# Wider small matmuls, three constant matmuls a chunk and later ScalarE routing calls in a fused RWKV and top-1 expert kernel

## The chip, the cores and the metric

The kernel runs on one core of a Trainium2 chip. The metric is the device time of one execution in microseconds (us). TensorE, VectorE, ScalarE, GpSimd (POOL) and the DMA issuer SP each run their own instruction stream in order and meet through semaphores.

## The reference

Two stages. The first is linear attention with a decaying state (RWKV) over r, k, v of shape (4 batches, 8 heads, 768 positions, 48), in float32:

```
for t in range(S):
    cur = einsum('bhd,bhe->bhde', u * k[t], v[t])
    y[t] = einsum('bhd,bhde->bhe', r[t], state + cur)
    state = w[:, None] * state + einsum('bhd,bhe->bhde', k[t], v[t])
```

The second takes y as x (3072 tokens of 384) into a mixture of 8 experts with one expert a token:

```
logits = x @ w_gate;  e = argmax(logits);  p = softmax(logits)[e]
o = sigmoid(x @ w_output_gate)[e]
out = p * o * (relu(x @ w1[e]) @ w2[e])      # w1: 384 x 1024, w2: 1024 x 384
```

## The kernel before, in words

The attention is cut into NT = 24 chunks of 128 positions: six steps in time, four batches in each, so that chunk i follows chunk i - 4 of its own batch. In a chunk the heads are held as four pairs; a chunk is split again into two halves of 64 positions, so nearly every matmul works on 64 by 64 or 48 by 64 corners of the 128 by 128 array, four of them (or two) side by side.

For one chunk these pieces of work exist, with the names that the code gives them:

- `load` (L1219): four DMAs on SP bring r, k (by head) and k, v (by token) into the tile `rkv`. `scale` (VectorE, L249), `keys` (POOL, L255) and `product` (POOL, L262) put the decay powers in.
- `scores` (L279): 16 float32 matmuls, 64 moving columns each, into columns 0 to 255 of the two banks `pa`. `causal` (VectorE, L285) masks them into `A`.
- `state` (L306): 16 matmuls with 48 moving columns, into columns 256 to 447 of the same two banks. `carry` (L316) adds the old state on VectorE (L323, or L320 for the first) and multiplies by the decay on POOL (L324): the tile `T`.
- `inter` (L340, 48 columns) and `intra` (L350, 48 columns) accumulate into the pair of banks `y`: what the state gives, and what the chunk itself gives. There is one pair, so the next chunk's `inter` waits for `output`.
- `coefs` (L360): eight matmuls, 128 rows by 64 columns of the array, whose moving operand repeats two columns 20 times: 40 columns. ScalarE copies eight of them out (`cs`, L1321), and `bonus` (L369) is eight ScalarE calls that multiply v by them.
- `output` (L376): VectorE adds y and the bonus to x; SP stores x. 
- `logits_t` (L413, three transposes of x into the one bank of tag `lg`, and ScalarE's copy `xT`, L415) and `logits_into` (L423): six matmuls whose moving operand repeats 16 gate columns three times, 48 in all. ScalarE copies 16 columns out (L431).

Each float32 matmul stands in the profile as two instructions.

The routing runs by groups of chunks (5, 5, 4, 4 and 6). `group` (L439) is a generator: it issues an operation or two and yields what kind of step comes next. In a chunk `micro` (L1306) is called at seven or more places; each adds a credit and lets VectorE steps run while credit lasts, and `tensor_slot` (L1313) lets a TensorE step run. The side generator `weighting` (L481) is advanced inside the same steps. ScalarE's three calls of a group are issued wherever the program is when it comes to them: the exponential `ex` (L464), the gate's exponential `en` (L492) and the row product `rhs` (L570). The last group runs after the attention, beside the first expert.

The order of every engine's stream in the attention is the order in which the code is written (`manual_schedule`). In the loop from L1354 one turn issues: product, scale, carry, keys, routing steps, the next chunk's `coefs` with ScalarE's copy, the logits of chunk i - 2, the transposes of x of chunk i - 1, the bonus calls of chunk i + 1, intra and output of chunk i, a load, state of chunk i + 2, scores of chunk i + 1, carry, causal, inter of chunk i + 1, routing steps. From chunk 18 on two pieces a turn split the first expert's weights on ScalarE and POOL (L798). Behind the loop come the experts, all on full 128 by 128 weights with up to 512 moving columns.

The kernel already holds a `warm` tile of bf16 ones, used for matmuls ahead of the attention (L114) and one in the loop's second turn (L1325).

Of the kernel before, what the change touches and what calls it, by code (L numbers as in the profile page):

```python
# [8 lines left out]
F32 = mybir.dt.float32  # L9
# [16 lines left out]
IN = RKW + 2 * DM  # L26
# [23 lines left out]
V, P, SPLIT = "vector", "tensor", "split"  # L50
# [3 lines left out]
BUDGETS = [[0, 0.25], [16, 0.3]]  # L54
# [177 lines left out]
class Attention:  # L232
    def __init__(self, tc, ctx, ps, k, load, x_d):
        self.tc, self.k, self.ps = tc, k, ps
        self.load, self.x_d = load, x_d
        self.pw = ctx.enter_context(tc.tile_pool(name="att_w", bufs=2))
        self.st, self.T, self.vc, self.A, self.rk, self.y = {}, {}, {}, {}, {}, {}
        self.pa = {}

    def view(self, i):  # L240
        t = self.load(i)
        return t[:, :RKW].rearrange("p (n c q t) -> p n c q t", n=2, c=2, q=NP), t[:, RKW : RKW + DM], t[:, RKW + DM :].rearrange("p (h d) -> p h d", h=H)
# [49 lines left out]
    def state(self, i):  # L292
        if i >= NT:
            return
        nc = self.tc.nc
        _, kn, vt = self.view(i)
# [14 lines left out]
    def carry(self, i, c):  # L311
        if i >= NT or (c == 1 and self.last(i)):
            return
        nc, k = self.tc.nc, self.k
        a = NP * HB
        U = self.pa[:, c, a : a + NP * D].rearrange("p (q e) -> p q e", q=NP)  # L316
        decay = k.w64.unsqueeze(2).to_broadcast((C, NP, D))
        T = self.pw.tile([C, NP, D], F32, name=f"T{c}", bufs=(3, B + 2)[c])
        if i < B and c == 0:
            nc.vector.tensor_mul(T, U, decay)  # L320
        else:
            T1 = self.pw.tile([C, NP, D], F32, name="Ts")
            nc.vector.tensor_add(T1, U, self.T[i, 0] if c else self.T[i - B, 1])  # L323
            nc.gpsimd.tensor_mul(T, T1, decay)  # L324
        self.T[i, c] = T

    def inter(self, i):
        if i >= NT:
            return
        nc = self.tc.nc  # L330
        rk = self.view(i)[0]
        self.y[i] = y = self.banks("ps_y", "y")
        T = [None if i < B else self.T[i - B, 1], self.T[i, 0]]
        for q in range(NP):
            for j in range(2):
                rows = slice(HB * j, HB * j + D)
                for c in range(2):
                    half = slice(HB * c, HB * (c + 1))
                    if T[c] is not None:
                        nc.tensor.matmul(y[half, j, D * q : D * (q + 1)], rk[rows, 0, c, q, :], T[c][rows, q, :], start=(q == 0), stop=False, skip_group_check=True)  # L340

    def intra(self, i):
        nc = self.tc.nc
        vt, A, y = self.view(i)[2], self.A.pop(i), self.y[i]
        for q in range(NP):
            for j in range(2):
                for c in range(2):
                    rows = slice(HB * c, HB * (c + 1))
                    o = y[rows, j, D * q : D * (q + 1)]
                    nc.tensor.matmul(o, A[rows, j, q, :], vt[rows, 2 * q + j, :], start=(i < B and c == 0 and q == 0), stop=(q == NP - 1), skip_group_check=True)  # L350

    def coefs(self, i, lg):
        if i >= NT:
            return
        rk = self.rk.pop(i)
        for q in range(NP):
            for n in range(2):
                half = slice(HB * n, HB * (n + 1))
                o = lg[half, : 60 * E].rearrange("p (a b) -> p a b", b=3 * E)[:, :, 2 * E + 2 * q : 2 * E + 2 * (q + 1)]
                self.tc.nc.tensor.matmul(o, rk[:, n, q, :], self.k.uw[:, q, :].unsqueeze(1).to_broadcast((C, 20, 2)), start=True, stop=True, skip_group_check=True)  # L360
# [11 lines left out]
    def output(self, i):  # L372
        nc = self.tc.nc
        x = self.pw.tile([C, DM], F32, name="x")
        xq, vq = (t.rearrange("p (q j) d -> p j q d", j=2) for t in (x.rearrange("p (h d) -> p h d", d=D), self.vc.pop(i)))
        nc.vector.tensor_add(xq, self.y.pop(i)[:, :, : NP * D].rearrange("p j (q d) -> p j q d", d=D), vq)  # L376
        nc.sync.dma_start(self.x_d[i * C : (i + 1) * C, :], x)
        return x


class Router:
# [36 lines left out]
    def logits_into(self, pl, xT):  # L418
        for j in range(KC):
            for n in range(2):  # L420
                half = slice(HB * n, HB * (n + 1))
                o = pl[half, : 9 * E].rearrange("p (a b) -> p a b", b=3 * E)[:, :, : 2 * E]
                self.tc.nc.tensor.matmul(o, xT[:, j, half], self.wg32[:, j, :].unsqueeze(1).to_broadcast((C, 3, 2 * E)), start=(j == 0), stop=(j == KC - 1), skip_group_check=True)  # L423
# [15 lines left out]
    def group(self, ps, w, lg, i0, G, closing, last):  # L439
# [24 lines left out]
        nc.scalar.activation(ex, d, AF.Exp)  # L464
# [16 lines left out]
        def weighting():  # L481
            z8 = mk("z8", E)
            nc.vector.tensor_mul(z8, oh, g)
            se = mk("se")
            nc.vector.tensor_reduce(out=se, in_=ex, axis=AX.X, op=ALU.add)
            yield
            z = mk("z")
            nc.vector.tensor_reduce(out=z, in_=z8, axis=AX.X, op=ALU.add)
            nc.vector.tensor_scalar(se, se, 1e-9, None, op0=ALU.add)
            yield  # L490
# [4 lines left out]
            yield  # L495
            den = mk("den")
            nc.vector.scalar_tensor_tensor(den, en, 1.0, se, op0=ALU.add, op1=ALU.mult)
            yield
            scale = self.scale[:, cols]
            nc.vector.reciprocal(scale, den)  # L500
            yield
            rest = scale
            for i in range(3):
                nc.vector.tensor_copy(parts[:, i], rest)
                yield
                if i < 2:
                    nxt = mk(f"rest{i}")
                    nc.vector.tensor_sub(nxt, rest, parts[:, i])
                    rest = nxt
                    yield  # L510
# [12 lines left out]
        next(side, None)  # L523
        yield V
# [10 lines left out]
        next(side, None)  # L535
        yield V
        rank = self.rank[:, cols]
        nc.vector.tensor_reduce(out=rank, in_=rk, axis=AX.X, op=ALU.add)
        next(side, None)
        yield V  # L540
        ge = mk("ge", NQ)
        nc.vector.tensor_tensor(ge, bc(rank, NQ), rep(k.thr, NQ), op=ALU.is_ge)
        next(side, None)
        yield V
        q = mk("q")
        nc.vector.tensor_reduce(out=q, in_=ge, axis=AX.X, op=ALU.add)
        next(side, None)
        yield V
# [4 lines left out]
        next(side, None)  # L553
# [8 lines left out]
        next(side, None)  # L562
# [3 lines left out]
        next(side, None)  # L566
# [3 lines left out]
        nc.scalar.activation(rhs[:, :, 1], sel, AF.Copy, scale=k.row1)  # L570
        tab = self.tab

# [17 lines left out]
        if last:  # L590
# [25 lines left out]
            for _ in weighting():  # L616
                yield V
# [15 lines left out]
        for _ in side:  # L633
            yield V
        for i in range(3):
            yield Slot(0.2)
            columns(i)
        yield P
# [559 lines left out]
def rwkv_top1_moe(ctx, tc, rkv, wu, wg, w1, w2, r, kk, v, w, u, out):  # L1198
# [11 lines left out]
    with ExitStack() as actx:  # L1210
# [105 lines left out]

        def strips(i, cs):
            if i < NT:
                lg = ps.tile([C, 512], F32, name="ps_cf", tag="lg", bufs=1)
                att.coefs(i, lg)  # L1320
                nc.scalar.copy(cs, lg[:, 2 * E : 3 * E])  # L1321
# [5 lines left out]
        make_tables(tc, ps, k)  # L1327
        att.scale(0)
# [25 lines left out]
        for i in range(NT):  # L1354
# [106 lines left out]
def laid_out(r, k, v, w, u, moe_w_gate, moe_w_output_gate, moe_w1, moe_w2):  # L1461
# [12 lines left out]
    for i, a in enumerate((w, u)):  # L1474
# [3 lines left out]
        "rkv": np.concatenate([heads(r), heads(k), tokens(k), tokens(v)], axis=2),  # L1478
# [27 lines left out]
```

## Time and profile before

| | us |
|---|---|
| median of three runs | 422.16 |
| lowest and highest of them | 419.49, 426.5 |
| the profiled execution | 421.16 |
| its span, first to last instruction | 419.2 |
| TensorE busy (matmul) in the span | 373.1 |
| VectorE, ScalarE, POOL busy | 234.9, 173.2, 156.3 |
| mean granted TensorE clock | 0.892 |

The span is the time from the first to the last instruction of the program; the profiled execution's own time is 1.96 us longer. The granted clock is the share of full speed that TensorE's clock was given: 1.00 is its level of 2.4 GHz and 0.50 its level of 1.2 GHz. In the profile's rows PE is TensorE's matmul stream and PEld its weight loads; DVE is VectorE, ACT ScalarE; `<-` names what ended an engine's wait, and "issue" is a wait that nothing in the profile explains. A matmul's end is modelled.

### The profile page before, as it was taken

How to read it: one execution, taken by the hardware profiler on the slowest of the kernel's cores; microseconds unless marked ns; L12 is line 12 of the kernel's file. 1: busy time of each engine (PE TensorE's matmuls, PEld its weight loads, DVE VectorE, ACT ScalarE, POOL GpSimd, SP SyncE). 2: the span in 40 equal slices, each digit the busy share in tenths (PEclk: the TensorE clock that was granted, in tenths of full speed). 3: DMA queues.
4: the chain of work that ended last, by engine and by line, in shares of the span. 5: the costliest groups of instructions: out<-in, count | busy, mean ns of one | idle time of the engine just before them, and what ended most of it. 6: DMA issues, size and time to landing. Idle time of an engine off the chain costs nothing. (4 is left out here: it accounts for less than half of the span.)

```text
span 419.2 us, 12629 instructions
## 1 busy us (share of the span) xinstructions
PE 373.1 (89%) x5134; PEld 354.6 (85%) x5134; DVE 234.9 (56%) x545; ACT 173.2 (41%) x481; POOL 156.3 (37%) x208
## 2 busy tenths in 40 slices
PE   5696967987787878999999999999999999999991
PEld 3686966886687768888989999999999999999990
DVE  5466478669769563265676246256264474534710
ACT  3354432635253343441345255255354453544500
POOL 4856437535634643532423042132321342402010
PEclk9999667869975555599999999999999999999997
DMA  7676545545736612306336346345364383643200
GB/s 242 201 240 218 182 145 187 175 158 187 236 118 212 216 55 77 96 2 193 103 101 218 96 116 210 104 143 179 108 204 162 115 263 96 201 156 121 85 34 25
DMA packets 30275, 62.66 MB, mean 149 GB/s; under 512 B 4223, under 2 KB 13491, under 8 KB 30208
## 3 DMA queue, kind: packets, MB, share of 16 engines
q1 hardware_dynamic: 26784, 51.95, 39.5%
q0 software_dynamic: 3424, 9.82, 7.0%
q8 instruction: 42, 0.69, 0.7%
q14 instruction: 25, 0.20, 0.2%
HBM read 52.31 MB, written 9.76 MB: 148 GB/s over the span
## 5 line engine op out<-in xcount | busy, mean ns | idle before, releaser
L891 POOL DMA_INDIRECT out_dram<-yo,si x28 | 29.9, 1068 | 131.2 <-ACT yo L888 72.4
L854 PE MATMUL ps_h<-xh,w1h 128*128 128x384 f32 (+4 forms) x216 | 72.7, 337 | 0.9 <-DVE yo L890 0.9
L856 PE MATMUL ps_h<-xh,w1l 128*128 128x384 f32 (+4 forms) x216 | 71.0, 329 | 0.0
L855 PE MATMUL ps_h<-xl,w1h 128*128 128x384 f32 (+4 forms) x216 | 71.0, 329 | 0.0
L803 DVE TENSOR_TENSOR w1l<-raw,w1h 128x768 fp32r<-128x768 f32 x28 | 26.1, 955 | 60.5 <-ACT w1h L802 60.5
L863 ACT ACTIVATE hh<-ps_h 128x384 fp32r<-128x384 f32 (+4 forms) x72 | 34.1, 475 | 45.0 <-PE ps_h L856 44.9
L864 DVE SCALAR_TENSOR_TENSOR hl<-ps_h,hh 128x384 fp32r<-128x384 f32 (+4 forms) x72 | 38.5, 535 | 22.1 <-ACT hh L863 21.9
L324 POOL TENSOR_TENSOR T<-Ts,sq 128x192 f32<-128x192 f32 x40 | 20.2, 506 | 71.6 <-DVE Ts L323 56.0
L825 POOL DMA_INDIRECT xg<-x_d,gi x28 | 31.0, 1106 | 41.3 <-PE ps_xt L837 25.7
L369 ACT ACTIVATE vc<-rkv,cs 128x48 f32<-128x48 f32 x192 | 45.9, 324 | 0.1
L916 PE MATMUL ps_o<-w2h,hh 128*128 128x384 f32 x128 | 43.7, 341 | 0.7 <-ACT yo L888 0.7
L918 PE MATMUL ps_o<-w2h,hl 128*128 128x384 f32 x128 | 42.8, 335 | 0.0
L917 PE MATMUL ps_o<-w2l,hh 128*128 128x384 f32 x128 | 42.8, 335 | 0.0
L854 PEld LDWEIGHTS ps_h<-xh,w1h 128*128 128x128 f32 x216 | 41.3, 191 | 1.4 <-issue 1.2
L350 PEld LDWEIGHTS ps_y<-rkv,A 64*64 64x64 f32 x768 | 33.9, 177 | 9.0 <-issue 8.3
L855 PEld LDWEIGHTS ps_h<-xl,w1h 128*128 128x128 f32 x216 | 41.3, 191 | 0.1
L856 PEld LDWEIGHTS ps_h<-xh,w1l 128*128 128x128 f32 x216 | 41.1, 190 | 0.1
L350 PE MATMUL ps_y<-rkv,A 64*64 64x48 f32 x768 | 37.7, 263 | 3.0 <-issue 3.0
L262 POOL TENSOR_TENSOR rk<-rkv 128x512 f32<-128x512 f32 x24 | 31.5, 1313 | 0.6 <-DMA rkv<-in_rkv_dram 0.6
L376 DVE TENSOR_TENSOR x<-ps_y,vc 128x384 f32<-128x384 f32 x24 | 13.3, 555 | 31.4 <-PE ps_y L350 19.5
L249 DVE TENSOR_TENSOR rkv<-rkv,ps_tb 128x1024 f32<-128x1024 f32 x24 | 29.0, 1212 | 0.7 <-ACT ps_tb L225 0.7
L803 DVE TENSOR_TENSOR w2l<-raw,w2h 128x768 fp32r<-128x768 f32 x28 | 26.8, 957 | 3.2 <-ACT w2h L802 2.0
(199 smaller groups left out, 739.6 us busy)
## 6 DMA issues: line engine op xcount, KB each, us to landing
raw<-in_w_dram SPq DMA_DIRECT2D x64, 384.0 KB, 3.4
rkv<-in_rkv_dram SPq DMA_DIRECT2D x48, 256.0 KB, 3.8
rkv<-in_rkv_dram SPq DMA_DIRECT2D x48, 192.0 KB, 4.2
x_d<-x SPq DMA_DIRECT2D x24, 192.0 KB, 2.9
xg<-x_d,gi POOLq DMA_INDIRECT x28, 3.5
out_dram<-yo,si POOLq DMA_INDIRECT x28, 2.7
wg<-in_wg_dram SPq DMA_DIRECT2D x1, 24.0 KB, 6.0
wu<-in_wu_dram SPq DMA_DIRECT2D x1, 4.0 KB, 1.7
```

Of the source, the lines that this page charges most:

```text
L262: self.tc.nc.gpsimd.tensor_mul(rk.rearrange("p c q t -> p (c q t)"), t[:, :512], t[:, 512:RKW])
L350: nc.tensor.matmul(o, A[rows, j, q, :], vt[rows, 2 * q + j, :], start=(i < B and c == 0 and q == 0), stop=(q == NP - 1), skip_group_check= ...
L369: nc.scalar.activation(vc[:, h, :], vt[:, h, :], AF.Copy, scale=cs[:, h : h + 1])
L803: (eng or nc.vector).tensor_sub(lo, self.raw[i][:, cs], hi)
L854: nc.tensor.matmul(o, wh[:, j, fs], xh, start=(j == 0), stop=False)
L855: nc.tensor.matmul(o, wh[:, j, fs], xl, start=False, stop=False)
L856: nc.tensor.matmul(o, wl[:, j, fs], xh, start=False, stop=(j == KC - 1))
L863: nc.scalar.activation(hh, o, AF.Relu)
L864: nc.vector.scalar_tensor_tensor(hl, o, 0.0, hh, op0=ALU.max, op1=ALU.subtract)
L916: nc.tensor.matmul(o, hh, wh, start=(f == 0), stop=False)
L917: nc.tensor.matmul(o, hh, wl, start=False, stop=False)
L918: nc.tensor.matmul(o, hl, wh, start=False, stop=(f == FC - 1))
```

## The change

All small matmuls get 64 moving columns. For `state` and `intra` the moving operand is 64 columns of v from the head's start on, 16 more than the head has; the last head needs 16 columns of padding, so `rkv` grows by PAD = 16 columns of zeros on the host's side. `inter` reads 64 columns of T in the same way; T's tiles are now nine fixed ones with 16 zeroed columns behind. In the banks a head pair now takes 64 columns, of which 48 are read. `coefs` repeats its two columns 32 times, `logits_into` its 16 four times.

A bank `spare` (the former bank of the logits, tag `l`) takes the logits in columns 0 to 63. `fill` is one bf16 matmul of the ones tile, 448 columns, into its columns 64 to 511; nobody reads them. It is issued three times a turn: behind the logits and their copy, ahead of `state`, and ahead of `inter` (the last turn has the first alone).

ScalarE's three calls of a group become steps of a kind of their own, `A`. `scalar_slot` lets one run: behind the transposes and the copy of x, behind the bonus calls, and near the turn's end. Until then the program stands still. The last group and the fallback path keep the old places. From chunk 19 on the credit is 0.4.

The diff, cut: constants and tiles, then `state`, `inter`, `group` and the loop. `intra` is edited as `state` is; in `coefs` 20 repeats become 32, in `logits_into` 3 become 4.

```diff
-IN = RKW + 2 * DM
+PAD = 16
+IN = RKW + 2 * DM + PAD
-BUDGETS = [[0, 0.25], [16, 0.3]]
+BUDGETS = [[0, 0.25], [16, 0.3], [19, 0.4]]
...
+        self.sums = [[self.pw.tile([C, NP * D + PAD], F32, name=f"T{c}_{n}", bufs=1) for n in range((3, B + 2)[c])] for c in range(2)]
+        for t in self.sums[0] + self.sums[1]:
+            tc.nc.gpsimd.memset(t[:, NP * D :], 0.0)
...
+    def values(self, i, rows, h):
+        return self.load(i)[rows, RKW + DM + h * D : RKW + DM + h * D + HB]
...
-                    o = pa[HB * j : HB * (j + 1), c, a + D * q : a + D * (q + 1)]
-                    nc.tensor.matmul(o, flat[rows, h * D : h * D + HB], vt[rows, h, :], start=True, stop=True, skip_group_check=True)
+                    o = pa[HB * j : HB * (j + 1), c, a + HB * q : a + HB * (q + 1)]
+                    nc.tensor.matmul(o, flat[rows, h * D : h * D + HB], self.values(i, rows, h), start=True, stop=True, skip_group_check=True)
...
-nc.tensor.matmul(y[half, j, D * q : D * (q + 1)], rk[rows, 0, c, q, :], T[c][rows, q, :], start=(q == 0), stop=False, skip_group_check=True)
+nc.tensor.matmul(y[half, j, HB * q : HB * (q + 1)], rk[rows, 0, c, q, :], T[c][rows, D * q : D * q + HB], start=(q == 0), stop=False, skip_group_check=True)
...
...
-        nc.scalar.activation(ex, d, AF.Exp)
+        if last or self.plain:
+            nc.scalar.activation(ex, d, AF.Exp)
...
-            yield
+            yield A
             en = mk("en")
             nc.scalar.activation(en, z, AF.Exp, scale=-1.0)
...
+        if not last and not self.plain:
+            yield A
+            nc.scalar.activation(ex, d, AF.Exp)
         yield P
...
-        nc.scalar.activation(rhs[:, :, 1], sel, AF.Copy, scale=k.row1)
...
+        yield A
+        nc.scalar.activation(rhs[:, :, 1], sel, AF.Copy, scale=k.row1)
         yield P
         pt = product(0, 5)
...
+        def scalar_slot():
+            if pend and pend[0][1] == A:
+                step()
+
+        def fill():
+            nc.tensor.matmul(k.spare[:, HB:], k.warm[:, :C], k.warm[:, HB:], start=True, stop=True, skip_group_check=True)
...
-                rt.logits_out(rt.logits_mm(ps, xTs.pop(i - 2), "l"), dst)
+                rt.logits_into(k.spare, xTs.pop(i - 2))
+                rt.logits_out(k.spare[:, : 2 * E], dst)
...
+            fill()
             if x is not None:
                 xTs[i - 1] = rt.logits_t(ps, rw, x, "lg", 1)
             else:
                 order_pe()
+            scalar_slot()
             att.bonus(i + 1, cs[(i + 1) % 2])
+            scalar_slot()
             tensor_slot(LAG)
...
+            if not tail:
+                fill()
             att.state(i + 2)
             att.scores(i + 1)
             att.carry(i + 2, 0)
             att.causal(i + 1)
+            if not tail:
+                fill()
             att.inter(i + 1)
             micro(i)
             tensor_slot(LAG)
             micro(i)
+            scalar_slot()
             micro(i)
```

## Rows read from the trace of the kernel before

**Rows 1.** Windows: stretch, us, busy PE, PEld, DVE, ACT, POOL, clock, DMA, GB/s.
```profile
20.30:174.50 154.20, 127.87 (x3528) 116.45 (x3522) 103.88 (x271) 66.06 (x270) 79.37 (x96) 0.74 0.54 169
...
93.00:113.40 20.40, 14.66 (x566) 13.10 (x560) 18.03 (x48) 8.22 (x36) 11.79 (x15) 1.00 0.62 192
...
23.40:27.40 4.00, 4.00 (x147) 3.63 (x145) 3.04 (x6) 2.63 (x11) 2.70 (x3) 1.00 0.80 238
```

**Rows 2.** Timeline of VectorE: start us, us, engine, line; four x adds.
```profile
24.75 0.56 DVE L376 TENSOR_TENSOR x<-ps_y,vc 128x384 f32<-128x384 f32 x1 [0.61 <-PE ps_y L350]
...
28.63 0.56 DVE L376 TENSOR_TENSOR x<-ps_y,vc 128x384 f32<-128x384 f32 x1 [0.62 <-ACT xT L415]
...
161.02 0.56 DVE L376 TENSOR_TENSOR x<-ps_y,vc 128x384 f32<-128x384 f32 x1 [1.36 <-PE ps_y L350]
...
167.94 0.56 DVE L376 TENSOR_TENSOR x<-ps_y,vc 128x384 f32<-128x384 f32 x1 [3.10 <-issue]
```

**Rows 3.** Windows again, of stretches at one granted clock each.
```profile
41.80:48.60 6.80, 6.80 (x160) 6.29 (x162) 1.16 (x5) 2.62 (x11) 1.57 (x3) 0.50 0.46 161
...
127.20:161.00 33.80, 27.10 (x514) 24.50 (x516) 23.12 (x72) 14.45 (x56) 17.32 (x20) 0.50 0.50 162
161.00:174.40 13.40, 13.40 (x258) 12.11 (x254) 4.98 (x17) 5.97 (x20) 7.48 (x8) 0.50 0.30 91
174.40:178.30 3.90, 3.90 (x27) 3.56 (x26) 0.56 (x1) 0.73 (x3) 1.14 (x3) 0.50 0.14 50
```

**Rows 4.** Waits of TensorE, 20 to 178 us: total us, times, longest.
```profile
PE ps_x L413 <- ACT cs L1321: 6.1, 5, 2.0
...
PE ps_y L350 <- issue: 3.0, 3, 2.0
PE ps_cf L360 <- issue: 2.5, 1, 2.5
...
PE ps_y L340 <- issue: 1.6, 1, 1.6
PE ps_l L423 <- issue: 1.2, 1, 1.2
```

**Rows 5.** Timeline of TensorE ahead of the falls at 55.5 and 113.5 us.
```profile
54.71 0.18 PE L518 MATMUL ps_c<-oh,tri 128*128 128x40 bf16 x1 [1.92 <-DVE oh L460]
...
113.83 0.76 PE L360 MATMUL ps_cf<-uw,rk 128*64 128x40 f32 x9 [2.45 <-issue]
```

**Rows 6.** Timeline of TensorE: state and scores of one turn.
```profile
124.33 0.68 PE L306 MATMUL ps_a<-rkv 64*64 64x48 f32 x32 [1.07 <-DVE Ts L323]
124.83 0.66 PE L279 MATMUL ps_a<-rkv 48*64 48x64 f32 x32
```

**Rows 7.** Windows again: 60 us of the expert stage.
```profile
300.00:360.00 60.00, 60.00 (x360) 59.66 (x360) 30.41 (x46) 28.16 (x51) 16.61 (x15) 1.00 0.52 163
```

**Rows 8.** Timeline of all engines: logits, transposes, ScalarE's logits copy, intra.
```profile
26.45 0.54 PE L423 MATMUL ps_l<-wg,xT 128*64 128x48 f32 x12
...
26.91 0.55 PE L413 MATMUL ps_x<-ident,x 128*128 128x128 f32 x3
27.03 0.17 ACT L431 COPY lg<-ps_l 128x16 f32<-128x16 f32 x1 [0.19 <-PE ps_l L423]
...
27.39 1.07 PE L350 MATMUL ps_y<-rkv,A 64*64 64x48 f32 x29
```

**Rows 9.** Waits of VectorE, 20 to 178 us.
```profile
DVE Ts L323 <- PE ps_a L279: 13.4, 18, 1.3
```

**Rows 10.** Waits of ScalarE, 20 to 180 us.
```profile
ACT en L492 <- DVE z L488: 10.6, 3, 5.7
ACT rhs L570 <- DVE rest L508: 8.0, 2, 4.1
```

**Rows 11.** Timeline of POOL ahead of the attention.
```profile
5.38 0.85 POOL L163 MEMSET caps<- 128x1 f32 x24
10.42 0.99 POOL L255 TENSOR_TENSOR rkv<-rkv,PK 128x384 f32<-128x384 f32 x1 [4.18 <-DMA rkv<-in_rkv_dram]
```

More of the change, by code (lines that the diff above doesn't have):

```diff
@@ L49 @@
 WARM = (4, 1)
-V, P, SPLIT = "vector", "tensor", "split"
+V, P, A, SPLIT = "vector", "tensor", "scalar", "split"
 SPLITS, SPLIT_AT = 2, 18
@@ L238, in __init__ @@
         self.pa = {}
+        self.sums = [[self.pw.tile([C, NP * D + PAD], F32, name=f"T{c}_{n}", bufs=1) for n in range((3, B + 2)[c])] for c in range(2)]
+        for t in self.sums[0] + self.sums[1]:
+            tc.nc.gpsimd.memset(t[:, NP * D :], 0.0)
     def view(self, i):
         t = self.load(i)
-        return t[:, :RKW].rearrange("p (n c q t) -> p n c q t", n=2, c=2, q=NP), t[:, RKW : RKW + DM], t[:, RKW + DM :].rearrange("p (h d) -> p h d", h=H)
+        return t[:, :RKW].rearrange("p (n c q t) -> p n c q t", n=2, c=2, q=NP), t[:, RKW : RKW + DM], t[:, RKW + DM : RKW + 2 * DM].rearrange("p (h d) -> p h d", h=H)
+    def values(self, i, rows, h):
+        return self.load(i)[rows, RKW + DM + h * D : RKW + DM + h * D + HB]
     def scale(self, i):
@@ L295, in state @@
         nc = self.tc.nc
-        _, kn, vt = self.view(i)
         flat = self.load(i)[:, RKW:]
@@ L315, in carry @@
         a = NP * HB
-        U = self.pa[:, c, a : a + NP * D].rearrange("p (q e) -> p q e", q=NP)
+        U = self.pa[:, c, a : a + NP * HB].rearrange("p (q e) -> p q e", q=NP)[:, :, :D]
         decay = k.w64.unsqueeze(2).to_broadcast((C, NP, D))
-        T = self.pw.tile([C, NP, D], F32, name=f"T{c}", bufs=(3, B + 2)[c])
+        flat = self.sums[c][i % len(self.sums[c])]
+        T = flat[:, : NP * D].rearrange("p (q e) -> p q e", q=NP)
         if i < B and c == 0:
@@ L322, in carry @@
             T1 = self.pw.tile([C, NP, D], F32, name="Ts")
-            nc.vector.tensor_add(T1, U, self.T[i, 0] if c else self.T[i - B, 1])
+            old = self.T[i, 0] if c else self.T[i - B, 1]
+            nc.vector.tensor_add(T1, U, old[:, : NP * D].rearrange("p (q e) -> p q e", q=NP))
             nc.gpsimd.tensor_mul(T, T1, decay)
-        self.T[i, c] = T
+        self.T[i, c] = flat
     def inter(self, i):
@@ L339, in inter @@
                     if T[c] is not None:
-                        nc.tensor.matmul(y[half, j, D * q : D * (q + 1)], rk[rows, 0, c, q, :], T[c][rows, q, :], start=(q == 0), stop=False, skip_group_check=True)
+                        nc.tensor.matmul(y[half, j, HB * q : HB * (q + 1)], rk[rows, 0, c, q, :], T[c][rows, D * q : D * q + HB], start=(q == 0), stop=False, skip_group_check=True)
     def intra(self, i):
         nc = self.tc.nc
-        vt, A, y = self.view(i)[2], self.A.pop(i), self.y[i]
+        A, y = self.A.pop(i), self.y[i]
         for q in range(NP):
@@ L348, in intra @@
                     rows = slice(HB * c, HB * (c + 1))
-                    o = y[rows, j, D * q : D * (q + 1)]
-                    nc.tensor.matmul(o, A[rows, j, q, :], vt[rows, 2 * q + j, :], start=(i < B and c == 0 and q == 0), stop=(q == NP - 1), skip_group_check=True)
+                    o = y[rows, j, HB * q : HB * (q + 1)]
+                    nc.tensor.matmul(o, A[rows, j, q, :], self.values(i, rows, 2 * q + j), start=(i < B and c == 0 and q == 0), stop=(q == NP - 1), skip_group_check=True)
     def coefs(self, i, lg):
@@ L358, in coefs @@
                 half = slice(HB * n, HB * (n + 1))
-                o = lg[half, : 60 * E].rearrange("p (a b) -> p a b", b=3 * E)[:, :, 2 * E + 2 * q : 2 * E + 2 * (q + 1)]
-                self.tc.nc.tensor.matmul(o, rk[:, n, q, :], self.k.uw[:, q, :].unsqueeze(1).to_broadcast((C, 20, 2)), start=True, stop=True, skip_group_check=True)
+                o = lg[half, : 32 * E].rearrange("p (a b) -> p a b", b=E)[:, :, 2 * q : 2 * (q + 1)]
+                self.tc.nc.tensor.matmul(o, rk[:, n, q, :], self.k.uw[:, q, :].unsqueeze(1).to_broadcast((C, 32, 2)), start=True, stop=True, skip_group_check=True)
     def bonus(self, i, cs):
@@ L375, in output @@
         xq, vq = (t.rearrange("p (q j) d -> p j q d", j=2) for t in (x.rearrange("p (h d) -> p h d", d=D), self.vc.pop(i)))
-        nc.vector.tensor_add(xq, self.y.pop(i)[:, :, : NP * D].rearrange("p j (q d) -> p j q d", d=D), vq)
+        nc.vector.tensor_add(xq, self.y.pop(i)[:, :, : NP * HB].rearrange("p j (q d) -> p j q d", d=HB)[:, :, :, :D], vq)
         nc.sync.dma_start(self.x_d[i * C : (i + 1) * C, :], x)
@@ L421, in logits_into @@
                 half = slice(HB * n, HB * (n + 1))
-                o = pl[half, : 9 * E].rearrange("p (a b) -> p a b", b=3 * E)[:, :, : 2 * E]
-                self.tc.nc.tensor.matmul(o, xT[:, j, half], self.wg32[:, j, :].unsqueeze(1).to_broadcast((C, 3, 2 * E)), start=(j == 0), stop=(j == KC - 1), skip_group_check=True)
+                o = pl[half, : 8 * E].rearrange("p (a b) -> p a b", b=2 * E)
+                self.tc.nc.tensor.matmul(o, xT[:, j, half], self.wg32[:, j, :].unsqueeze(1).to_broadcast((C, 4, 2 * E)), start=(j == 0), stop=(j == KC - 1), skip_group_check=True)
     def logits_mm(self, ps, xT, tag):
@@ L485, in weighting @@
             nc.vector.tensor_reduce(out=se, in_=ex, axis=AX.X, op=ALU.add)
-            yield
+            yield V
             z = mk("z")
@@ L489, in weighting @@
             nc.vector.tensor_scalar(se, se, 1e-9, None, op0=ALU.add)
-            yield
+            yield A
             en = mk("en")
@@ L494, in weighting @@
                 expert()
-            yield
+            yield V
             den = mk("den")
             nc.vector.scalar_tensor_tensor(den, en, 1.0, se, op0=ALU.add, op1=ALU.mult)
-            yield
+            yield V
             scale = self.scale[:, cols]
             nc.vector.reciprocal(scale, den)
-            yield
+            yield V
             rest = scale
@@ L504, in weighting @@
                 nc.vector.tensor_copy(parts[:, i], rest)
-                yield
+                yield V
                 if i < 2:
@@ L509, in weighting @@
                     rest = nxt
-                    yield
+                    yield V
         parts = None if last else w.tile([C, 3, G], BF16, name=f"parts_{G}", tag="parts")
         side = iter(()) if last else weighting()
+        if not last and not self.plain:
+            yield A
+            nc.scalar.activation(ex, d, AF.Exp)
         yield P
@@ L522, in group @@
             nc.tensor.matmul(cnt[:, (c + 1) * E :], k.ones16, oh16[:, c, :].unsqueeze(1).to_broadcast((C, G - 1 - c, E)), start=False, stop=(c == G - 2), skip_group_check=True)
-        next(side, None)
-        yield V
+        yield next(side, V)
         rk = mk("rk", E)
@@ L534, in group @@
             nc.vector.tensor_copy(self.csum16, self.csum)
-        next(side, None)
-        yield V
+        yield next(side, V)
         rank = self.rank[:, cols]
         nc.vector.tensor_reduce(out=rank, in_=rk, axis=AX.X, op=ALU.add)
-        next(side, None)
-        yield V
+        yield next(side, V)
         ge = mk("ge", NQ)
         nc.vector.tensor_tensor(ge, bc(rank, NQ), rep(k.thr, NQ), op=ALU.is_ge)
-        next(side, None)
-        yield V
+        yield next(side, V)
         q = mk("q")
         nc.vector.tensor_reduce(out=q, in_=ge, axis=AX.X, op=ALU.add)
-        next(side, None)
-        yield V
+        yield next(side, V)
         pp = mk("pp")
@@ L552, in group @@
         nc.vector.tensor_tensor(eqq, bc(q, NQ), rep(k.ip[:, :NQ], NQ), op=ALU.is_equal)
-        next(side, None)
+        yield next(side, V)
         yield Slot(0.2)
@@ L561, in group @@
         )
-        next(side, None)
+        yield next(side, V)
         yield Slot(0.6)
@@ L565, in group @@
         nc.vector.tensor_tensor(ohp, bc(pp, QP), rep(k.ip, QP), op=ALU.is_equal)
-        next(side, None)
+        yield next(side, V)
         yield Slot(0.3)
@@ L569, in group @@
         (nc.vector if last else nc.gpsimd).tensor_mul(rhs[:, :, 0], sel, bc(k.tile0[:, cols], W))
-        nc.scalar.activation(rhs[:, :, 1], sel, AF.Copy, scale=k.row1)
         tab = self.tab
+        if last:
+            nc.scalar.activation(rhs[:, :, 1], sel, AF.Copy, scale=k.row1)
         def columns(i):
@@ L615, in group @@
             parts = w.tile([C, 3, G], BF16, name=f"parts_{G}", tag="parts")
-            for _ in weighting():
-                yield V
+            yield from weighting()
             for i in range(3):
@@ L632, in group @@
             return
-        for _ in side:
-            yield V
+        yield from side
         for i in range(3):
@@ L637, in group @@
             columns(i)
+        yield A
+        nc.scalar.activation(rhs[:, :, 1], sel, AF.Copy, scale=k.row1)
         yield P
@@ L1320, in strips @@
                 att.coefs(i, lg)
-                nc.scalar.copy(cs, lg[:, 2 * E : 3 * E])
+                nc.scalar.copy(cs, lg[:, :E])
         def order_pe():
@@ L1327, in rwkv_top1_moe @@
         make_tables(tc, ps, k)
+        k.spare = ps.tile([C, 512], F32, name="spare", tag="l", bufs=1)
         att.scale(0)
@@ L1477, in laid_out @@
     return {
-        "rkv": np.concatenate([heads(r), heads(k), tokens(k), tokens(v)], axis=2),
+        "rkv": np.concatenate([heads(r), heads(k), tokens(k), tokens(v), np.zeros((NT, C, PAD), np.float32)], axis=2),
         "wu": wu.reshape(C, 2, NP),
```

## The prediction

> **What bounds the kernel now.** I read the windows by stage first. From the first store of x (20.3 us) to the last (174.5) the kernel works through its chunks: 23 chunk periods in 154.2 us, 6.70 us each, with TensorE busy 127.87 us and VectorE 103.88 us, at a mean granted clock of 0.74 [rows 1]. Everything behind is 245 us of expert work at the full clock that the change does not touch. Then the distance between two x adds, the once-a-chunk marker: 3.88 us at the high level (2.4 GHz) and 6.92 us at the low one (1.2 GHz), both without routing work [rows 2]. In such a chunk TensorE is busy 4.00 of 4.00 us while VectorE has 3.04 us to do [rows 1]: TensorE sets the pace and its clock scales it. Where a group's routing runs, VectorE does: 18.03 of 20.4 us busy against TensorE's 14.66 at the high level [rows 1].
>
> So the clock is what is to be had. At a mean of 0.74 the stage spends (1 - 0.74) x 2 x 154.2 = 80 us at the low level: five pieces of 6.8 us like the first of [rows 3], and from 127.2 to the end. Ahead of the falls TensorE had idled: 1.92 us for a routing one-hot, 2.45 us for nothing that the profile shows [rows 5], and 1.0 to 2.0 us in the other four. It sat idle 154.2 - 127.87 = 26.3 us in all: 8.3 us "issue" in six gaps, 6.1 us ahead of the x transposes for ScalarE's coefficient copy [rows 4], the rest for VectorE. Being busy alone does not bring the level back: from 161.0 to 174.4 TensorE had not one idle moment, all in matmuls of 40 to 64 columns on half of the array or a quarter, and stayed at 0.50; it rose after 3.9 us of full-array matmuls of 256 columns [rows 3]. That speaks for wider moving operands and for fills on the whole array.
>
> **The change part by part.** Of a chunk at the high level that TensorE bounds; base 4.1 us (3.88, and 16 more matmuls from the fifth chunk on, at 0.50 us for 32 [rows 6]).
>
> 64 columns. The nearest row is the scores' own: in one burst, at one clock, 32 matmuls with 48 columns take 0.68 us and 32 with 64 columns 0.66 us [rows 6]. So nothing for state and inter, which use the same four tiles. For intra, coefficients and logits, with two tiles, no row has 64; lower bound 0, upper bound in proportion to the columns: a third of what is neither transposes (0.48 us [rows 8]) nor scores (0.50), 1.0 us. I take 0.2, near the row.
>
> Three fills. In 60 us of the expert stage, busy throughout at the high level, 360 matmuls of full weights ran, most of 384 columns [rows 7]: 0.167 us each, and 0.2 for 448. Into and out of full-array work the next group starts 0.07 to 0.08 us ahead of the last one's recorded end (logits, transposes, intra [rows 8]), where tiled groups overlap by 0.18 [rows 6]: 0.1 us a switch. The first fill stands ahead of the transposes, where that switch is made already; the other two add a way in and a way out each. 3 x 0.2 + 4 x 0.1 = 1.0 us; bounds 0.6 (columns alone) and 1.4 (0.2 a switch). The Trainium skill, "TensorEngine Tiling (Array Packing)", Key Properties, has it that changing the tiling mode drains the engine; without that rule the fills would cost the 0.6, with it the 1.0 that I take. The rows above show the smaller overlap.
>
> The first fill's wait. It writes columns 64 to 511 of the bank whose first 16 ScalarE's logits copy reads, right ahead of it in order. Today the transposes start at 26.91; that copy runs from 27.03 to 27.20 [rows 8]. If order is kept by bank, TensorE starts 0.3 us later in each chunk; if by address, 0; if ScalarE is held up, 0.5 or more. I take 0.3: carry's add, which reads state's columns alone, is released by the scores that follow in the same bank, 18 times [rows 9]. Behind the waiting fill stand the transposes, intra and so x. The Trainium skill, "PSUM — Partial Sum Buffer", in its section on bank collisions, asks to guard PSUM by bank and quadrant, not by address; by that rule the sum has the 0.3 (13 x 0.3 = 3.9 us over the light chunks), by address it has none. The trace agrees, with the 18 releases.
>
> ScalarE's calls moved. Today the exponential `en` waits 10.6 us in three cases and the row product 8.0 us in two, in order, ahead of the coefficient copy [rows 10]; that is most of TensorE's 6.1 us ahead of the transposes. Behind the x copy they hold up only the eight bonus calls, needed a chunk later. The 6.1 us lie in routing chunks, where VectorE is late next: I count no gain from them, beyond making the 0.3 above hold. What a routing program pays is a pause until the next ScalarE place, at three points of a group; the budget of 0.4 from chunk 19 catches it up.
>
> Nothing on the path: nine more memsets on POOL, some 0.3 us at the rate of 24 in 0.85, lie in its 4.18 us wait for the first load [rows 11]; SP issues as many loads as before, one of them 4% longer; the strided reads of y and U have the same element counts.
>
> A light chunk: 4.1 + 0.2 + 1.0 + 0.3 = 5.6 us. Of the 23 I take 10 as routing chunks (four groups, two to three each); with 3.04 us in a light one these have (103.88 - 13 x 3.04) / 10 = 6.4 us of VectorE work, which covers TensorE's 5.6. Stage: 13 x 5.6 + 10 x 6.4 = 136.8; plus half of the 8.3 us "issue" gaps, the slower stream covering the rest, 4; plus one fall to the low level, 3: **143.8 us** instead of 154.2. The 3.9 us at the low level up to 178.3 lose half, 2. The profiled execution took 421.16 us (span 419.2, 1.96 around it), 1.0 us under the median of the runs shown: 421.16 - 10.4 - 2 = 408.8, so **409 us**.
>
> **The rivals.**
> 1. *Clock held, gain eaten by TensorE's own stream.* All six "issue" gaps lie in stretches at the high level, none in the 80 us at the low one. If twice the time at the high level brings twice the gaps, 16.6 us instead of 4, the result is 409 + 12 = **421 us**. For: the count. Against: the longer chunk leaves the stream more time.
> 2. *Slower: the clock still falls.* At the low level a chunk would take 6.92 plus twice 1.2 for fills and columns less their overlaps, say 9.1 us, against a mean of 5.95 (136.8 / 23). Each us at the low level then costs 3.15 / 9.1 = 0.35 us; above 35 us the gain is gone, above some 60 us it is slower by 2%. With today's share of 52%: 23 chunks take 23 / (0.52 / 9.1 + 0.48 / 5.95) = 167, plus 4: 171 us, so **438 us**. For: the waits ahead of the falls (a one-hot from VectorE, "issue") all stay, and a fill of 0.2 us fills little of 2. Against: [rows 3], where wide matmuls brought the level back.
> 3. *The change holds the clock only in part:* the short falls stay, 30 us at the low level instead of 8: 409 + 0.35 x 22 = **417 us**.
>
> On the low side: if the pauses for ScalarE spread the routing over more chunks, so that VectorE stays under 5.6 us, all 23 take about 5.6 us: 129 + 4 + 3 = 136, and 401 us; with the fills at their lower bound and no wait, 396.
>
> **How the numbers follow.** Forecast 0.50 (399 to 414), rival 1 0.15, rival 3 0.20, rival 2 0.15. Two per cent of the median are 8.4 us, about what a measurement of this kernel can tell, so faster means under 413.7: nearly all of the forecast and a little of rival 3, 0.50; within, 0.36; slower, 0.14. The upper bounds of fills and columns (1.4 and 1.0, a light chunk of 6.8) give 409 + 13 x 1.2 + 10 x 0.4 = 429. Range 399 to 428; the forecast's own is 399 to 414.
>
> **What would show it.** The x adds 5 to 6 us apart where no routing runs; a granted clock over 0.9 from 20 to the last x; logits, wait for ScalarE's logits copy, fill, transposes in this order, with some 0.3 us idle ahead of the fill; state, scores and inter as long as now; no `en` ahead of a coefficient copy. Wrong if light chunks take under 5 us (fills or waits were priced too high), if "issue" gaps pass 12 us, or if the low level holds for more than 35 us.

## The result and the profile after

The changed kernel takes 406.9 us (median of four runs, 406.02 to 408.18) against 421.4 us for the kernel before beside it: a ratio of 0.967, 95% interval 0.962 to 0.972, so 3.3% faster. The forecast was 409, the range 399 to 428. The profiled execution took 407.04 us with a span of 405.3. In this document medians are over all runs of a kernel, while ratios leave out the runs that came out over 1.5% above the fastest of the same kernel.

The page of the changed kernel, in 40 slices; each digit is the busy share, or the granted clock, of a slice in tenths. The recorded clock has one dent in the stage of chunks, where the kernel before spent 81.5 us at the low level:

```profile
span 405.3 us, 12777 instructions
...
PE   5799978997998887899999999999999999999990
...
PEclk9999999999999989999999999999999999999997
```

Windows of the changed kernel (columns as in [rows 1]): 9.5 us around the first x add, the whole stage of chunks, its one recorded piece at the low level, and what lies behind the last x add.

```profile
17.90:27.40 9.50, 9.25 (x153) 7.26 (x154) 2.90 (x5) 3.16 (x15) 4.25 (x5) 1.00 0.38 120
...
20.40:161.00 140.60, 124.33 (x3603) 101.30 (x3603) 105.26 (x272) 65.76 (x270) 77.88 (x95) 0.99 0.59 186
...
143.60:146.90 3.30, 3.04 (x42) 2.47 (x40) 3.30 (x15) 1.85 (x7) 2.48 (x3) 0.50 0.06 23
161.00:405.30 244.30, 232.01 (x1413) 226.94 (x1413) 120.74 (x240) 100.12 (x188) 64.20 (x60) 0.99 0.42 131
```

The first row shows that 1.00 is not always a measured clock. The trace's clock record begins at 27.5 us, and the windows count what lies ahead of it as full. But there TensorE is busy 9.25 us with 153 instructions, where the light chunk from 28.16 on needs 5.00 us for 147; and a fill takes 0.55 us, as it does at the recorded low level (0.53 at 145.0 us), against 0.35 at the high one. So this execution ran the first 7 us of the stage at the low level as well: its first chunk takes 7.73 us, against 4.81 in a second trace of the same kernel.

The stage went from 154.2 [rows 1] to 140.6 us, and all of the gain is there: behind the last x it was 244.6 and is 244.3. TensorE's busy time fell by 3.5 us although the fills came in, because some 10 us run at the low level instead of 81.5; its idle time fell from 26.3 to 16.3. Waits of TensorE in the stage of the changed kernel, to be laid beside [rows 4]:

```profile
PE spare L1330 <- ACT lg L439: 5.7, 18, 0.7
PE ps_y L348 <- DVE x L384: 4.3, 4, 1.5
...
PE ps_c L530 <- DVE oh L468: 1.4, 1, 1.4
PE spare L1330 <- ACT last_lg L439: 1.1, 4, 0.3
...
PE ps_a L286 <- issue: 0.9, 2, 0.5
PE ps_cf L368 <- issue: 0.2, 1, 0.2
```

The wait for the coefficient copy (6.1 us) is gone, and so is most of two that the prediction did not single out: the waits of the table product `ps_tab` for VectorE's `rhs` (all 4.0 us) and of the counts `ps_c` for `oh` (1.9 of 3.3). In the kernel before these were:

```profile
PE ps_tab L579 <- DVE rhs L574: 4.0, 4, 2.3
PE ps_c L518 <- DVE oh L460: 3.3, 2, 1.9
```

The "issue" gaps went from 8.3 to 1.1 us. New are 22 waits of the first fill for the logits copy, 6.8 us.

Timeline of the changed kernel: two x adds a light chunk apart, to be laid beside [rows 2] (3.88 us there), and the logits, their copy, the first fill and the transposes of the next one, beside [rows 8]:

```profile
28.16 0.56 DVE L384 TENSOR_TENSOR x<-ps_y,vc 128x384 f32<-128x384 f32 x1 [3.03 <-PE ps_y L358]
...
33.43 0.56 DVE L384 TENSOR_TENSOR x<-ps_y,vc 128x384 f32<-128x384 f32 x1 [1.59 <-ACT xT L423]
...
36.07 0.52 PE L431 MATMUL spare<-wg,xT 128*64 128x64 f32 x12
...
36.63 0.17 ACT L439 COPY lg<-spare 128x16 f32<-128x16 f32 x1 [0.18 <-PE spare L431]
...
36.86 0.35 PE L1330 MATMUL spare<-warm 128*128 128x448 bf16 x1 [0.27 <-ACT lg L439]
37.05 0.49 PE L421 MATMUL ps_x<-ident,x 128*128 128x128 f32 x3
```

The adds are 5.27 us apart, and four more periods take 5.11 to 5.30; four of 4.78 to 5.03 each stand behind a longer one. The fill stands 0.27 us behind the copy, in the order that the prediction named. So light chunks became slower, as forecast, and the stage became shorter all the same.

### The profile page after: what moved, and what is told of

Read it like the earlier page. It is cut to its first block, busy times and chain, and to the rows that moved or that the text cites. A ratio compares the mean times of both kernels' runs of the same rounds, so it can differ in the third digit from the quotient of the medians.

```text
span 405.3 us, 12777 instructions
## 1 busy us (share of the span) xinstructions
PE 369.1 (91%) x5204; PEld 337.7 (83%) x5204; DVE 236.5 (58%) x545; ACT 173.2 (43%) x481; POOL 155.9 (38%) x217
## 5 line engine op out<-in xcount | busy, mean ns | idle before, releaser
L811 DVE TENSOR_TENSOR w1l<-raw,w1h 128x768 fp32r<-128x768 f32 x28 | 26.1, 954 | 60.8 <-ACT w1h L810 60.8
L833 POOL DMA_INDIRECT xg<-x_d,gi x28 | 30.6, 1094 | 40.0 <-PE ps_xt L845 24.5
L1330 PE MATMUL spare<-warm 128*128 128x448 bf16 x70 | 26.0, 372 | 6.8 <-ACT lg L439 5.7
L358 PEld LDWEIGHTS ps_y<-rkv,A 64*64 64x64 f32 x768 | 25.9, 142 | 5.0 <-issue 3.4
L358 PE MATMUL ps_y<-rkv,A 64*64 64x64 f32 x768 | 29.2, 229 | 0.0
```

Source lines behind the costliest of these rows:

```text
L358: nc.tensor.matmul(o, A[rows, j, q, :], self.values(i, rows, 2 * q + j), start=(i < B and c == 0 and q == 0), stop=(q == NP - 1), skip_gro ...
L811: (eng or nc.vector).tensor_sub(lo, self.raw[i][:, cs], hi)
```

## The experiments

**Each part taken back.** The theory on record: wide operands and fills hold the clock, and moving ScalarE's calls is worth nothing by itself. Its rival: fills cost what they give. All three kernels here start from the changed one.

Without the three fills:

```diff
-            fill()
...
-            if not tail:
-                fill()
...
-            if not tail:
-                fill()
```

> The changed kernel without its three constant matmuls a chunk; 64 columns and the moved ScalarE calls stay. Theory A (the fills hold the clock): the clock falls again, over 30 us of the attention stage at 0.50, and the time goes back to 412 to 425 us. Theory B (64 columns and fewer waits hold it by themselves): a granted clock over 0.97 from 28 us to the last x, light chunks of 4.3 to 4.6 us instead of 5.3, and 393 to 400 us.

407.34 us, ratio 0.967 (0.958 to 0.975): the same as with them. Windows and waits of TensorE in this kernel:

```profile
20.40:160.80 140.40, 109.81 (x3530) 98.04 (x3522) 103.39 (x272) 66.11 (x270) 78.32 (x95) 0.91 0.59 187
```

```profile
PE ps_y L348 <- DVE x L384: 7.0, 5, 3.0
PE spare L431 <- issue: 2.7, 2, 1.5
PE ps_a L286 <- issue: 2.5, 2, 1.3
PE ps_y L348 <- issue: 2.2, 2, 1.2
PE ps_cf L368 <- issue: 2.1, 1, 2.1
PE ps_y L358 <- issue: 1.7, 2, 1.1
PE ps_a L312 <- issue: 1.6, 1, 1.6
```

The light chunk is 3.92 us instead of 5.27, and over the stage TensorE is busy 14.5 us less. It is given back: TensorE's idle time grows by 14.3 us, from 16.3 to 30.6, with 12.8 us of "issue" gaps instead of 1.1, and 25.5 us are recorded at the low level, in pieces of 3.4 to 6.9, instead of 3.4. Every run shows the lower clock: a mean of 0.944 to 0.960 over the program, against 0.977 to 0.989 in ten runs of the changed kernel. So beside the moved calls the fills do hold the clock, and what they give goes in full into their own time.

The old moving columns, 48 and 40, the same in every small matmul:

```diff
-        return self.load(i)[rows, RKW + DM + h * D : RKW + DM + h * D + HB]
+        return self.load(i)[rows, RKW + DM + h * D : RKW + DM + h * D + D]
...
```

> The changed kernel with the old moving columns (48 in state, inter, intra and logits, 40 in the coefficients); the fills and the moved ScalarE calls stay. Theory A (the fills hold the clock): clock over 0.97 in the stage, chunks as long as with 64 columns or up to 0.2 us shorter, 402 to 407 us. Theory B (the 64 columns are what holds it): over 20 us at 0.50 and 412 us or more.

412.35 us, 0.976 (0.964 to 0.987). Until 144.5 us its periods are close to those of the changed kernel. Then the clock falls at the same place, and it stays low longer; windows of this kernel:

```profile
20.30:144.50 124.20, 110.53 (x3296) 91.00 (x3296) 94.99 (x240) 56.76 (x238) 67.60 (x84) 1.00 0.63 198
144.60:165.00 20.40, 19.86 (x305) 16.03 (x305) 9.77 (x32) 9.36 (x32) 10.67 (x12) 0.50 0.26 80
```

20.4 us at the low level against 3.3 in the changed kernel. These are one trace of each. Over all runs the mean granted clock is 0.950 to 0.968 with the old columns, against 0.977 to 0.989, while the intervals of the two times overlap. So the wider columns cost no time that shows, and with them less of the program runs at the low level.

ScalarE's calls in their old places:

```diff
-        if last or self.plain:
-            nc.scalar.activation(ex, d, AF.Exp)
+        nc.scalar.activation(ex, d, AF.Exp)
...
-            yield A
+            yield V
...
-        if last:
+        if True:
             nc.scalar.activation(rhs[:, :, 1], sel, AF.Copy, scale=k.row1)
...
-        yield A
-        nc.scalar.activation(rhs[:, :, 1], sel, AF.Copy, scale=k.row1)
```

> The changed kernel with ScalarE's three routing calls of a group back in their old places; fills and 64 columns stay. My theory: the clock is held all the same, but the calls stand ahead of the logits copy, for which the first fill waits: five to eight waits of 1 to 4 us in routing chunks, mostly where VectorE is late as well, so 407 to 413 us. Rival (the waits of ScalarE are what let the clock fall): over 20 us at 0.50, 415 us or more.

426.27 us, 1.012 (1.003 to 1.021): some 19 us lost, slower than the kernel before. This was the part counted at nothing. Windows and waits of TensorE in this kernel:

```profile
20.40:179.00 158.60, 132.52 (x3603) 107.73 (x3603) 107.47 (x272) 65.97 (x270) 78.70 (x95) 0.90 0.52 164
```

```profile
PE spare L1324 <- ACT lg L439: 7.6, 18, 1.7
PE ps_tab L583 <- DVE rhs L578: 7.5, 4, 2.4
PE spare L1324 <- ACT last_lg L439: 3.7, 4, 2.9
PE ps_c L526 <- DVE oh L468: 2.6, 2, 1.4
```

The largest wait that came back is not for ScalarE but for VectorE's last column of `rhs`, and 30.7 us run at the low level. Fills and 64 columns are both in this kernel, so they do not hold the clock by themselves.

**One part alone.** Both kernels keep the credit of 0.4 from chunk 19. The moved calls alone are the changed kernel with the first two edits above together:

> Of the change the moved ScalarE calls alone (with the padding, the new credit and the bank of the logits): no fills, old columns. Theory C (the moved calls are the main part, fills and columns each do little beside them): 405 to 413 us. Theory D (64 columns or fills are needed as well, or the low clock stays on once it has come): pieces of over 10 us at 0.50 and 414 to 421 us.

411.43 us, 0.984 (0.977 to 0.991). Windows, then waits of TensorE:

```profile
20.30:164.90 144.60, 126.74 (x3529) 115.03 (x3522) 104.75 (x272) 66.27 (x270) 78.84 (x96) 0.75 0.57 181
```

```profile
PE ps_c L530 <- DVE oh L468: 1.5, 1, 1.5
PE ps_x L421 <- ACT cs L1336: 1.2, 3, 0.5
```

The stage is 9.6 us shorter than [rows 1] at nearly the same clock, 0.75 against 0.74. Most of that is TensorE's idle time, 17.9 us instead of 26.3. By the waits: the coefficient copy -4.9, `rhs` -4.0, `oh` -1.8, "issue" -2.6, and the waits for carry, for x and for `csum` +4.7.

The 64 columns alone are the first edit above and the third:

> Of the change the 64 columns alone (with the padding, the new credit and the bank of the logits): no fills, ScalarE's calls in their old places. Theory C (the moved calls are the main part): ScalarE's waits of 1 to 3 us ahead of the transposes stay, 417 to 427 us. If the columns by themselves are the main part: under 413 us.

417.48 us, 0.994 (0.989 to 0.999): the low level lasts 47.8 us instead of 81.5, the waits stay (6.0 for the coefficient copy, 5.7 for `rhs`, 3.0 for `oh`). One low piece lasts 20.5 us here, so 64 columns alone do not make such pieces short. Beside the moved calls the columns are worth more: the kernel without fills above is this change and the calls together, 0.967 against 0.984 for the calls alone, with 25.5 us at the low level instead of 71.0.

**Place or pause?** Moving the calls does two things: ScalarE gets them at another place, and the routing program stands still until that place comes. This kernel issues them in their old places and keeps the pauses:

```diff
-            yield A
+            yield V
             en = mk("en")
             nc.scalar.activation(en, z, AF.Exp, scale=-1.0)
+            yield A
...
             yield A
-            nc.scalar.activation(ex, d, AF.Exp)
...
```

> The changed kernel with ScalarE's three calls issued in their old places, but the routing program still pausing there until the next ScalarE place. If the place in ScalarE's stream is what matters (the calls stand ahead of the coefficient and logits copies and hold up the fill): 418 to 427 us, as without the move. If the pause is what matters (it spreads VectorE's routing work over more chunks): 406 to 412 us.

409.26 us, 0.979 (0.972 to 0.986). Of the 19 us, 17 by the medians, 14 by the ratios, are there with the pause alone. Its waits of TensorE:

```profile
PE spare L1328 <- ACT lg L439: 6.8, 18, 1.6
PE ps_y L348 <- DVE x L384: 4.2, 5, 1.2
PE spare L1328 <- ACT last_lg L439: 3.5, 4, 1.9
PE ps_c L529 <- DVE oh L468: 1.4, 1, 1.4
```

The wait for `rhs` is gone; the fill waits longer for ScalarE than in the changed kernel (10.3 us against 6.8), and 10.2 us are recorded at the low level. The place is worth what is left, 2 to 5 us.

That gave a new theory: TensorE's routing steps stood too early in its order. A TensorE step, `P` in the code, is issued when `micro` has been called LAG times since the program reached it, and with 2 the VectorE work that it needs is still queued, so that TensorE, in order, stands in front of it with all of the attention behind. If so, one constant replaces the pause. From the kernel with the calls in their old places:

```diff
-LAG = 2
+LAG = 5
```

> The kernel with fills, 64 columns and ScalarE's calls in their old places (426 us before this edit), with one constant changed: the routing's TensorE steps are issued at the earliest five routing places after they are reached, instead of two. Theory E (the pauses help because the counts and the table product come later in TensorE's order, when VectorE is done; in their old place TensorE waited 7.5 us for the product's operand and 2.6 us for the one-hot): those waits under 3 us together, and 406 to 414 us. Rival (ScalarE's calls themselves, by holding up the copies and the fill): the fill's waits stay over 9 us and the time at 418 to 427 us.

409.02 us, 0.981 (0.970 to 0.993), against 426.27. Windows, then waits of TensorE:

```profile
20.20:162.20 142.00, 122.48 (x3603) 99.88 (x3603) 103.91 (x272) 66.08 (x270) 79.00 (x96) 0.98 0.57 185
```

```profile
PE spare L1324 <- ACT lg L439: 6.7, 18, 1.3
PE ps_xt L839 <- DMA xg<-x_d,gi: 4.5, 2, 3.8
PE ps_y L348 <- DVE x L384: 2.9, 3, 1.2
PE spare L1324 <- ACT last_lg L439: 2.2, 4, 1.4
```

The waits for `rhs` and `oh` are gone, the clock is 0.98, and ScalarE's calls still stand where they stood. The later steps are paid for at the stage's end: the first gather of tokens comes later, 4.5 us. The two stages differ by 16.6 us: TensorE idles 6.6 us less (19.5 instead of 26.1; `rhs` 7.5, `oh` 2.6 and the fill's 2.4 less, the gather 4.5 more, and smaller ones), and is busy 10.0 us less with the same 3603 instructions, of which 24.8 us fewer run at the low level. In the trace with 2 each of the five falls of the clock, at 59.2, 76.3, 110.4, 141.1 and 154.8 us, comes during or behind a wait for `oh` or `rhs`; these waits end at 57.4, 74.5, 109.6, 142.2 and 151.5. With 2 the four products start 0.05 us behind the last column of `rhs`, with 5 they start 1.2 to 1.65 us behind it. One thing the constant does not part: while a TensorE step is held back the routing program stands still, so VectorE's later steps come later as well, as with the pause.

The same constant in the kernel before, with the changed kernel's credit:

```diff
-BUDGETS = [[0, 0.25], [16, 0.3]]
+BUDGETS = [[0, 0.25], [16, 0.3], [19, 0.4]]
...
-LAG = 2
+LAG = 5
```

> The kernel before with the same constant at five and the credit of 0.4 from chunk 19: no fills, old columns, ScalarE's calls in their old places. Theory E: TensorE's 4.0 and 3.3 us of waits for the product's operand and the one-hot go, and the time falls to 409 to 415 us, as with the moved calls alone. Rival (the waits only move to ScalarE's copies and to x): 417 to 423 us.

415.18 us, 0.991 (0.986 to 0.997), in between the two expectations. The trace is of the fastest of ten runs, 408.32 us. Waits of TensorE:

```profile
PE ps_xt L837 <- DMA xg<-x_d,gi: 5.1, 2, 4.3
PE ps_x L413 <- ACT cs L1321: 4.1, 5, 1.8
```

`rhs` and `oh` no longer hold TensorE up; the coefficient copy and the late gather do, and 44.9 us stay at the low level. So without fills and wide columns the constant gives about 1%, and there the place of ScalarE's calls counts too: with them moved the wait for the coefficient copy is 1.2 us.

**The first fill's wait.** The fill goes between the logits and their copy, so that it has nothing to wait for:

```diff
                 rt.logits_into(k.spare, xTs.pop(i - 2))
+                fill()
                 rt.logits_out(k.spare[:, : 2 * E], dst)
...
-            fill()
+            if i < 2:
+                fill()
```

> The changed kernel with the first fill ahead of ScalarE's logits copy in order instead of behind it, so that it has nothing to wait for. My theory: the 0.27 us that TensorE waits in each chunk goes away, light chunks 5.3 to 5.0 us, 14 to 22 times: 401 to 404 us. Rival (the wait is covered: ScalarE's copy, now behind the fill, or VectorE sets the pace anyway): within 1 us of 406.9.

406.04 us, 0.969 (0.960 to 0.978): no difference from the changed kernel that these runs show, although the light chunk falls from 5.27 to 4.94 us. In the same place with the fill ahead of `state` left out as well:

```diff
-            if not tail:
-                fill()
             att.state(i + 2)
```

> The changed kernel with the first fill ahead of ScalarE's logits copy and without the fill ahead of state: two fills a chunk. If a fill costs its 0.3 us in a light chunk: light chunks of 4.6 to 4.8 us and 398 to 403 us. If shorter chunks only bring the issue gaps and falls of the clock back, as without any fill: 404 to 409 us, with over 5 us of issue gaps or over 10 us at 0.50.

403.46 us, 0.962 (0.954 to 0.970). Both this kernel and the changed kernel ran again, on one chip:

> The version with two fills, the first ahead of ScalarE's logits copy, beside the changed kernel on the same chip, to see whether it is the faster of the two. If the shorter chunk is worth what its stage showed: 401 to 405 us and 2 to 5 us under the changed kernel. If issue gaps and falls of the clock take it back: within 2 us of it.

> The changed kernel as it is, again, as the yardstick for the version with two fills: 405 to 409 us, with one or two short pieces at 0.50 and under 2 us of issue gaps.

402.69 us, 0.968 (0.959 to 0.977), and 406.26, 0.975 (0.967 to 0.983). Over ten runs each the medians are about 3.5 us apart, in the same direction both times, but the intervals overlap: likely 1% faster, not settled. The changed kernel's second trace has two pieces of 3.4 us at the low level and 2.0 us of "issue" gaps. x adds of the two-fill kernel in its second series, and its stage:

```profile
25.53 0.56 DVE L384 TENSOR_TENSOR x<-ps_y,vc 128x384 f32<-128x384 f32 x1 [1.10 <-PE ps_y L358]
...
30.02 0.56 DVE L384 TENSOR_TENSOR x<-ps_y,vc 128x384 f32<-128x384 f32 x1 [1.25 <-ACT xT L423]
```

```profile
20.40:156.00 135.60, 116.37 (x3576) 97.64 (x3569) 105.33 (x272) 66.31 (x270) 78.47 (x95) 0.96 0.61 193
```

Its light chunk is 4.49 us; part of that comes back as "issue" gaps (5.3 us) and as low level (11.2 us).

## Why the prediction was right, and where it was not

- *What bounds the kernel, the clock:* held for the light chunk, where TensorE is busy 5.00 of 5.27 us and VectorE 2.90. A routing chunk is no longer bound by VectorE alone: in the longest, of 8.83 us, VectorE is busy 7.33 and TensorE 7.16. One reading ahead of it was wrong: from 161.0 to 174.4 us 3.3 of TensorE's 13.4 us were 128-column matmuls on the whole array (`L413`, `L837`), not only narrow ones on parts of it, and the clock stayed low all the same.
- *The sum, 143.8 us for the stage:* 140.6, and that it is so near is in part luck. The 13 shortest chunks average 5.27 us instead of 5.6, the ten longest 7.2 instead of 6.4, and the 4 and 3 us for gaps and the fall, added on top in the sum, lie within them. Errors of 4, 8 and 7 us nearly cancel. Three chunks came under the 5 us that were named as a sign of being wrong. One of them, 4.94 us, takes as long in the kernel with the moved calls alone, so the fills cost nothing there.
- *64 columns, 0.2 us a light chunk (0 to 1.0):* the same period is 3.92 us with them and without fills, 3.88 before: 0.04. The row that it was nearest to was right, and the proportional bound far off. Right as well that the columns help the clock, by the runs with the old ones.
- *Three fills 1.0, the wait 0.3:* by that period 3.92 without fills, 4.49 with two, 4.94 with three, the first ahead of the copy, 5.27 in the changed kernel: 1.02 and 0.33. The fills cost more than the 0.6 us that the prediction estimated for their columns. The Trainium skill, "TensorEngine Tiling (Array Packing)", Key Properties, has a change of the tiling mode drain the engine; that fits, but no run here separates the drain from the rest.
- *Order by bank:* the 22 waits are there and go when the fill stands ahead of the copy. The fill writes other columns than the copy reads, and waits for a semaphore all the same. The Trainium skill, "PSUM — Partial Sum Buffer", on bank collisions, asks for such a guard by bank and quadrant, not by address; the trace agrees, in that this program has it. What happens without it no run shows.
- *ScalarE's calls moved, no gain beyond making the 0.3 hold:* wrong, and the largest error. Alone the calls are worth some 7 us (4 to 10 by the ratio's interval), beside fills and columns 19. The prediction looked at what ScalarE's queue held up and priced that at nothing. It wrote of the pause as a cost to the program; beside fills and columns it is the pause that pays, and one constant that brings the TensorE steps later does nearly the same.
- *The clock held by fills:* right that they hold it, if the waits are gone too (with ScalarE's calls in their old places 30.7 us are low in spite of them), wrong that this is where the gain is; without them the time is the same. The gain of the whole change is there with calls and columns alone, 0.967. In the sum one gain too many (the fills') stood in place of one left out (the pauses'). Fills alone were not run.
- *"Issue" gaps, half of them stay, 4 us:* 1.1 us. Rival 1, more of them at the high level, happens where the fills are absent (12.8 us), not here. Rivals 2 and 3 did not come: 3.4 us recorded at the low level, one fall as forecast, and the 7 us ahead of the record.
- *Behind the last x, -2 us:* -0.3. The low level there is gone, but ScalarE is late next. Timeline of the changed kernel at the stage's end:

```profile
162.82 1.75 ACT L810 CAST w2h<-raw 128x384 fp32r<-128x384 f32 x4
...
164.47 0.48 ACT L423 COPY xT<-ps_x 128x384 f32<-128x384 f32 x1
...
165.00 0.57 PE L431 MATMUL ps_l<-wg,xT 128*64 128x64 f32 x12 [0.75 <-ACT xT L423]
```

Four casts of the second expert matrix stand ahead of the last x copy, and the last logits wait 0.75 us for it. That the whole 1.7 us went this way is not shown.

Two things stay open: what an "issue" gap is (shown is only that it comes with short light chunks and goes with fills), and why less time is spent at the low level with 64 columns (3.3 us against 20.4 behind the same fall, in one trace of each).

## What to carry to other kernels

Before pricing a moved call, list what else moves with it: here the steps of another, in-order engine that come behind it, and the first question should be whether those steps stand where their inputs are ready. A filler that raises a clock has to be weighed by its own time: leaving it out altogether is the first experiment, not the last.

## What the hardware showed that was not expected

- Waits of TensorE can cost twice: of the 16.6 us that one constant gave, 6.6 are idle time of TensorE and 10.0 are busy time of the same instructions, with 24.8 us less at the low level.
- 64 instead of 48 or 40 moving columns on a quarter or half of the array are nearly free (3.92 against 3.88 us a chunk).
- A granted clock of 1.00 at the start of a trace can mean that no record exists yet: in the changed kernel's the record begins at 27.5 us, and the fills ahead of it take 0.55 us, as at the low level.
- The shorter the light chunk, the longer TensorE stands still for nothing that the profile shows: 12.8 us in the stage with chunks of 3.92 us, 5.3 with 4.49, 1.1 with 5.27. What these gaps are is not shown.
